# Reordering column turns, SyncE's requests and row loads in one layer of an attention and MLP kernel

## Chip, cores and metric

The kernel runs on one core of one Trainium2 chip. The metric is the device time of one launch in microseconds, the median of several runs; lower is better.

## What is computed

A routed attention block is followed by a small MLP with a layer norm and a residual sum. Only the second half matters here:

```python
B, H, S, D = 4, 8, 768, 64                  # x: (4, 768, 512)
x  = attention(q, k, v, centroids)          # softmax within clusters, per head
mu  = mean(x, -1); var = mean((x - mu)**2, -1)
xn  = (x - mu) / sqrt(var + 1e-6) * g_ln
out = x + maximum(xn @ w_ch1, 0) @ w_ch2    # w_ch1: 512 x 2048, w_ch2: 2048 x 512
```

Everything is in float32.

## The kernel before

The attention of all four sequences comes first and takes the span up to about 318 us. Then the MLP runs sequence by sequence, numbered b = 0 to 3. Matrix products are split with Strassen's method (seven products of half blocks instead of eight), the later ones twice over, so that between the products there are many sums and differences on VectorE.

The MLP's first layer of one sequence goes in eight **units**, j = 0 to 7, written by `first_units(b, j)` followed by `unit_end(b, j)`. A unit is a list of seven **parts** in the order 1, 2, 4, 6, 3, 5, 7, each one product of four matmuls with 128x384 results; parts 4 and 3 belong to the unit before. Parts 1, 6, 7 and 4 collect in one PSUM bank, `x_ps`: ScalarE copies its state out (`p1` after part 1, `u2` after part 6, `u3` after part 7, by `kept`, line 881) before the next part adds to it. Part 6 can therefore not start before the copy p1 is done, nor part 7 before u2. VectorE adds these copies to other banks (line 886), and ScalarE then applies the relu (line 894). In part 4 ScalarE applies the relu straight from the bank (line 923).

All five engines here take their instructions in the order in which the code issues them (a schedule written out by hand; SyncE, which issues most DMAs, included). So an instruction that waits holds up everything behind it on its engine.

Much else is tucked into the units of b = 1 and the stretch after it:

- **Rows of x for sequence 2.** `rows_load(2, t)` (line 560) fetches 128 rows of x (256 KB) from DRAM into a tile `xr`, of which there are two. `norm_rows(2, t)` (lines 573 to 575) lets ScalarE find their mean and spread. This is done at the ends of units 0 to 5, and each call requests the row block two further on once its own tile is free. From these, `norm_stats` and `norm_stat_rows` (at the ends of units 5 and 6) make the layer norm's factors: a small store `stat_d` to DRAM, and after it two loads that spread it over all partitions, `stat_row`.
- **Columns of x for sequence 3.** x lies in DRAM by columns. `columns_load` fetches 384 KB of it into `col` (line 534). `columns_turn` lets VectorE transpose it (line 518) and puts four stores of 96 KB into a list, `leaving`; they go to DRAM row by row in pieces of 128 bytes. `leave(n)` issues the first n of that list (line 1224). Turns stand at the ends of units 0, 2 and 4, loads at the ends of 1 and 3. Loaded and transposed tile share one pair of buffers.
- **Splits of the second weight.** At the end of each unit but the last, `w2_split(m, ...)` makes four differences on VectorE (line 1068) and stores 1 MB to DRAM, `w_d` (line 1069). `w2_back(i)` fetches 1 MB of earlier sums, `w_t`, at the ends of units 1, 3 and 4 (line 1047).
- **The ring.** The second layer ("deep" products, line 1151) takes its 49 weights of 256 KB, from `w_d`, `w_t` and `w_all`, through a ring of ten buffers. `ring_load` issues a load (line 1093); at the ends of units 5, 6 and 7 up to four each. The first products are named (4,1), (4,2), (4,6), (4,5), (4,7), (7,1) and so on.

The order in `unit_end` before the change is: row work, four of the leaving stores, the split with its store, `w2_back`, pending jobs, `norm_stats` and `norm_stat_rows`, leaving stores, column turn or load, ring loads. The same functions serve b = 2, whose first layer uses smaller products and takes about 13 us per unit; its row work already stands behind part 1.

Of the kernel before, what the change touches and what calls it, by code (L numbers as in the profile page):

```python
# [23 lines left out]
def kernel(  # L24
# [11 lines left out]
    nc = tc.nc  # L36
    B, H, S, D = q.shape
# [3 lines left out]
    NT = S // P  # L41
# [501 lines left out]
    rows = {}  # L543
# [11 lines left out]
            nc.sync.dma_start(out=xn[:, c, :], in_=xT_d[b][c])  # L555

    def rows_load(b, t):
        if t < NT:
            x = (ffn if b else last).tile([P, DM], F32, tag="xr", name="xr", bufs=2 + (not b))
            nc.sync.dma_start(out=x, in_=x_d[b][t])  # L560
            rows[b, t] = x

    def norm_rows(b, t):
        if b < 2:
            rows_load(b, t + 2 - b)
        x = rows.pop((b, t))
        if t == 0:
            moments[b] = small.tile([P, NT, 3], F32, tag="mv", name="mv")
        mv = moments[b]
        if b != 1:  # L570

            total, mean = mv[:, t, 0:1], mv[:, t, 1:2]
            nc.scalar.activation(x, x, AF.Identity, accum_out=total)
            nc.scalar.mul(mean, total, -1.0 / DM)
            nc.scalar.activation(x, x, AF.Square, bias=mean, accum_out=mv[:, t, 2:3])
            if b:
                rows_load(b, t + 2)
            return
        bn = small.tile([P, 6], F32, tag="bn", name="bn")
        nc.vector.bn_stats(out=bn, in_=x)  # L580
        nc.vector.bn_aggr(out=mv[:, t, :2], in_=bn)
# [350 lines left out]
    def by_half(w):  # L932

        return w.rearrange("p c (h f) -> p h c f", h=2)
# [126 lines left out]
    def w2_split(m, src):  # L1061

        blocks = [[src[:, j, l * NQH : (l + 1) * NQH] for j in range(2)] for l in range(2)]
        (b11, b12), (b21, b22) = blocks
        t = splits.tile([P, 4, NQH, P], F32, tag="wt", name="wt", bufs=2)
        t1, t2, t3, t4 = [t[:, i] for i in range(4)]
        for o, x, y in ((t1, b12, b11), (t2, b22, t1), (t3, b22, b12), (t4, b21, t2)):
            nc.vector.tensor_tensor(o, x, y, ALU.subtract)  # L1068
        nc.sync.dma_start(
            out=w2_d[ORDER.index(m)].rearrange("w p f -> p w f"), in_=t.rearrange("p w c f -> p w (c f)")  # L1070
        )

# [149 lines left out]
    def leave(n, queues=(nc.sync,)):  # L1222
        for i, (to, y) in enumerate(leaving[:n]):
            queues[i % len(queues)].dma_start(out=to, in_=y)
        del leaving[:n]
# [378 lines left out]
    def first_units(b, j):  # L1604

        chunks = within.pop(j, []) if b == 0 else []
        parts = ((1, 0), (2, 0), (4, 1), (6, 0), (3, 1), (5, 0), (7, 0))
        sums_after, inner_at = 5, {}
        if b >= PAIRED:
            parts = ((1, 0), (5, 0), (4, 1), (6, 0), (3, 1), (7, 0))  # L1610
            sums_after, inner_at = 3, {5: (7,), 6: (4, 3)} if j % 2 else {6: (1, 2), 7: (6, 5)}
            if j == 1:
                inner_at = {1: (1, 2), 6: (6, 5), 3: (7,), 7: (4, 3)}
        for part, ahead in parts:
            if chunks and part in (1, 3):
                split_weight(chunks[0])
            if j >= ahead:
                first_layer(b, j - ahead, part)
            if part in (4, 6, 3):
                relu(1)  # L1620
            if part in inner_at:
                inner_products(pairs_of[b, j - j % 2], inner_at[part])
                if 3 in inner_at[part]:
                    summed.extend(hidden_tile(0, j - i) for i in (1, 0))
                relu(len(summed))
            if inner_at and part == 1 and j % 2 == 0:
                if j == 2:
                    outer_sums(0, True)
                pair_begin(b, j)
            if inner_at and part == 1 and b + 1 < B and j < NT:  # L1630
                norm_rows(b + 1, j)
            if chunks and part in (2, 3):
                m = chunks.pop(0)
                join_weight(m)
                load_weight(m + RAWS)

            if part == sums_after and j + 1 < NFH:
                w1_sums(b, j + 1)
                if inner_at:
                    outer_keep(b, j + 1)  # L1640
            if inner_at and j % 2 and part in (1, 5):
                inner_keep(b, j - 1, {1: 5, 5: 3}[part])
            if part == sums_after and b and j:
                if not inner_at or j % 2 and j > 1:
                    outer_sums(j - 1, b > 1 or j > 4)
                if j + 1 == NFH and not inner_at:
                    inner_sums(deep[b], ORDER[0], cs=slice(0, NQH - 1))
            if inner_at and part == 7 and j % 2 == 0:
                outer_sums(j - 1, True)
# [82 lines left out]
    with tc.manual_schedule(engines=order | {mybir.EngineType.SP}):  # L1732
        first.close()
        splits = first.enter_context(tc.tile_pool(name="splits", bufs=1))
        outer = {}

        def unit_end(b, j):

            if b + 1 < B:
                if j == 0 and b < PAIRED:  # L1740
                    rows_load(b + 1, 1)
                if j < NT and (b < PAIRED or j == 0):
                    norm_rows(b + 1, j)
            if b == 1:
                leave(4)
                if j == 0:
                    outer["ends"] = all_in_range()
                if j == 2:
                    outer["flag"] = flag_of(outer.pop("ends"))
                m = (1, 5, 3, 4, 2, 7, 6, None)[j]  # L1750
                if m in SUMS:
                    w2_split(m, outer.pop(("t", SUMS.index(m) + 1)))
                elif m:
                    w2_split(m, by_half(w2_block(*{1: (0, 0), 2: (1, 0), 3: (1, 1)}[m])))
                if j in (1, 3, 4):
                    w2_back({1: 4, 3: 3, 4: 2}[j])
                if j in (5, 6):
                    outer_late("s", "e", (0, 0), j - 5)
            while pending:
                job = pending.pop(0)  # L1760
                if job is None:
                    break
                job()
            if b + 1 < B and j + 3 == NFH:
                norm_stats(b + 1)
            if b + 1 < B and j + 2 == NFH:
                norm_stat_rows(b + 1)
            leave(8 if b >= PAIRED else 4)
            if b == 1:
                if turning and j % 2 == 0:  # L1770
                    columns_turn(row, lambda out, in_: leaving.append((out, in_)))
                elif asked and j % 2:
                    columns_load(row)
            if j > 4:
                for _ in range(4):
                    if ring["next"] < len(STEPS) * (b - 1) + RING:
                        ring_load(b)

        for b in range(1, B):
            deep[b] = {}  # L1780
            if b + 1 < B:
                rows_load(b + 1, 0)
                if b >= PAIRED:
                    rows_load(b + 1, 1)
            if b == 1:
                w2_back(1)
                first_units(b, 0)
            elif b == LAST:
                last_load(3, 0)
                last_layer(b)  # L1790
            else:
                first_layer(b, 0, 6)
                w1_sums(b, 0, (2, 3))
                x_sum(b, 3)
                first_layer(b, 0, 5)
                x_sum(b, 4)
                first_layer(b, 0, 7)
                w1_sums(b, 1)
                deep_room(b)
                outer_keep(b, 0)  # L1800
                outer_keep(b, 1)
                pair_begin(b, 0)
            if b < LAST:
                unit_end(b, 0)
                for j in range(1, NFH):
                    first_units(b, j)
                    unit_end(b, j)
                relu(len(summed))
            if b == LAST:
                pass  # L1810
            elif b >= PAIRED:
                inner_sums(deep[b], ORDER[0], cs=slice(0, NQH - 1))
            else:
                inner_sums(deep[b], ORDER[0], cs=slice(NQH - 1, NQH))
            if b == 1:
                first.close()
                units = pool("units", 1)
            deep_layer(b, b + 1 < B, deep[b])
        flag = outer["flag"]
# [231 lines left out]
```

## Time and profile before

| What | us |
|---|---|
| Median of 3 runs | 879.64 |
| Lowest and highest run | 879.08, 880.81 |
| The profiled execution's own time | 880.61 |
| Its span, first to last instruction | 878.8 |
| TensorE (PE) busy in the span | 866.9 |
| VectorE (DVE) busy | 730.0 |
| ScalarE (ACT) busy | 408.0 |

In lines of the profile, PE is TensorE's matmuls, PEld its weight loads, DVE VectorE, ACT ScalarE, SP SyncE; a q after the name means the engine's sequencer, as for all DMA requests. A line of the timeline gives start, duration, engine, source line, operation, the tiles written and read, the shapes, and in brackets how long the engine had been idle and what ended that. A line of the waits gives who waited for whom, the sum in us, how often, and the longest. The first layer of b = 1 lies between 464 and 536 us, the second layer after it up to about 602 us.

### The profile page before, as it was taken

What the parts mean: (1) busy time and instruction counts of PE and PEld (TensorE: products, weight loads), DVE (VectorE), ACT (ScalarE), POOL (GpSimd) and SP (SyncE); (2) the same over time, 40 slices, a digit from 0 to 9 for tenths busy, and PEclk for the clock granted to TensorE, in tenths of its full rate; (3) what the DMA queues carried; (4) which work ended last, traced back from release to release, by engine and by line L of the source; (5) the groups of instructions that cost most, each with busy time, mean ns of one, the idle gap of its engine ahead of it and who ended that gap; (6) DMA issues with size and microseconds to landing.
All of it is one profiled execution on the core that took longest, in us unless ns stands there. A gap on an engine that the chain in (4) does not pass through costs nothing.

```text
span 878.8 us, 13640 instructions
## 1 busy us (share of the span) xinstructions
PE 866.9 (99%) x4744; PEld 586.4 (67%) x4744; DVE 730.0 (83%) x1262; ACT 408.0 (46%) x758; POOL 77.6 (9%) x143
## 2 busy tenths in 40 slices
PE   8999999999999999999999999999999999999996
PEld 5444444444444445568886557997667998778996
DVE  6899999999999888959667778897877897867875
ACT  6777788888888833330004452102553111443110
POOL 1012121222222212110000000000000000000000
PEclk9999999999999999999999999999999999999999
DMA  7777789999987328876685787965557875464875
GB/s 153 147 130 128 146 174 193 196 210 198 187 176 193 104 83 222 238 187 230 182 195 158 223 276 271 324 193 143 141 173 251 291 203 153 126 179 136 274 200 110
DMA packets 258493, 164.68 MB, mean 187 GB/s; under 512 B 192992, under 2 KB 211440, under 8 KB 257392
## 3 DMA queue, kind: packets, MB, share of 16 engines
q1 hardware_dynamic: 227392, 144.43, 60.7%
q0 software_dynamic: 7776, 15.03, 8.7%
q10 hardware_dynamic: 23248, 4.25, 2.8%
q8 instruction: 40, 0.66, 0.3%
q14 instruction: 37, 0.30, 0.1%
HBM read 115.21 MB, written 40.07 MB: 177 GB/s over the span
## 4 chain that ended last, share of the span: by engine, by line
PE 91%; DVE 3%; DMA 3%; ACT 1%; issue 1%; ACTq 0%; SPq 0%; DVEq 0%
PE s_ps L401 18%; PE x_ps L855 17%; PE a_ps L413 14%; PE x_ps L1151 11%; PE z_ps L855 6%; PE z_ps L1151 5%; PE x_ps L964 5%; PE y_ps L1151 3%; PE x_ps L1274 2%; PE z_ps L964 2%; PE y_ps L855 2%; PE sim_ps L320 1%; PE den_ps L469 1%; PE z_ps L1274 1%; PE y_ps L964 1%; DVE wt L1068 1%
## 5 line engine op out<-in xcount | busy, mean ns | idle before, releaser
L401 PE MATMUL s_ps<-t,t 64*128 64x384 f32 x768 | 154.8, 483 | 0.0
L401 PEld LDWEIGHTS s_ps<-t,t 64*128 64x128 f32 x768 | 68.0, 187 | 39.0 <-issue 38.3
L1151 PE MATMUL x_ps<-lower,w 128*128 128x192 f32 x448 | 80.8, 326 | 0.9 <-DVE u L1166 0.5
L1151 PEld LDWEIGHTS x_ps<-lower,w 128*128 128x128 f32 x448 | 74.1, 190 | 2.2 <-DVE u L1166 0.7
L396 ACT ACTIVATE e<-s_ps 128x768 f32<-128x768 f32 x84 | 67.1, 812 | 7.0 <-PE s_ps L401 6.4
L396 ACT ACTIVATE w<-s_ps 128x768 f32<-128x768 f32 x80 | 64.4, 813 | 8.3 <-PE s_ps L401 7.7
L894 ACT ACTIVATE lower<-lower 128x384 f32<-128x384 f32 x88 | 43.7, 520 | 51.8 <-DVE lower L886 37.7
L401 PE MATMUL s_ps<-mask,mask 64*128 64x384 bf16 x384 | 62.8, 323 | 1.0 <-ACT e L396 0.6
L881 ACT COPY u<-x_ps 128x384 f32<-128x384 f32 x64 | 30.6, 478 | 61.1 <-PE x_ps L855 61.0
L413 PE MATMUL a_ps<-e,v_sb 128*64 128x384 f32 x336 | 57.6, 488 | 0.0
L881 ACT COPY p<-x_ps 128x384 f32<-128x384 f32 x32 | 15.1, 473 | 86.5 <-PE x_ps L855 81.4
L413 PE MATMUL a_ps<-w,v_sb 128*64 128x384 f32 x320 | 55.2, 488 | 0.0
L855 PE MATMUL x_ps<-xt,ws 128*128 128x384 f32 x128 | 46.8, 488 | 0.9 <-ACT p L881 0.9
L855 PE MATMUL x_ps<-xn,w 128*128 128x384 f32 x128 | 46.6, 487 | 0.0
L855 PE MATMUL x_ps<-xn,ws 128*128 128x384 f32 x128 | 46.6, 487 | 0.0
L855 PE MATMUL x_ps<-xt,w 128*128 128x384 f32 x128 | 46.5, 486 | 0.0
L413 PEld LDWEIGHTS a_ps<-e,v_sb 128*64 128x64 f32 x336 | 23.5, 137 | 31.8 <-issue 29.3
L1506 POOL DMA_DIRECT2D out_dram<-y_end x2 | 1.2, 596 | 483.8 <-DVE y_end L1502 483.8
L413 PEld LDWEIGHTS a_ps<-w,v_sb 128*64 128x64 f32 x320 | 22.4, 137 | 30.4 <-issue 27.5
L401 PEld LDWEIGHTS <-mask 64*128 64x128 bf16 x384 | 18.9, 94 | 35.0 <-issue 10.0
L1164 ACT COPY u<-x_ps 128x192 f32<-128x192 f32 x30 | 9.6, 319 | 64.6 <-PE x_ps L1151 60.1
L886 DVE TENSOR_TENSOR lower<-z_ps,u 128x384 f32<-128x384 f32 x40 | 22.2, 555 | 20.6 <-PE z_ps L855 12.5
(296 smaller groups left out, 1834.7 us busy)
## 6 DMA issues: line engine op xcount, KB each, us to landing
w<-w_d SPq DMA_DIRECT2D x84, 256.0 KB, 3.3
raw<-in_moe_w_ch_dram SPq DMA_DIRECT2D x32, 512.0 KB, 4.5
w<-w_t SPq DMA_DIRECT2D x36, 256.0 KB, 5.4
w<-tb POOLq DMA_DIRECT2D x32, 256.0 KB, 5.7
w_d<-wt SPq DMA_DIRECT2D x7, 1024.0 KB, 5.9
w<-w_all SPq DMA_DIRECT2D x27, 256.0 KB, 3.0
v_sb<-in_v_dram SPq DMA_DIRECT2D x32, 192.0 KB, 3.6
xr<-x_d SPq DMA_DIRECT2D x24, 256.0 KB, 3.2
```

Source lines behind the costliest of these rows:

```text
L320: nc.tensor.matmul(sim[r : r + Q, :HC], cT[:, pr, :, :].rearrange("p j c -> p (j c)"), prepared[n][side][:, g * HC : (g + 1) * HC], start= ...
L396: nc.scalar.activation(e, s[:, :, :HC], AF.Exp, scale=SCALE)
L401: nc.tensor.matmul(s[:, j, :HC], of_keys[:, keys], of_queries[:, o : o + HC], start=part == first, stop=part != first, skip_group_check=True,)
L413: nc.tensor.matmul(acc[j * D : (j + 1) * D, :HC], loaded[n]["v"][:, j, c, :], e[:, j, :], start=(c == 0), stop=(c == NT - 1),)
L855: nc.tensor.matmul(bank[:, :HC], lhs[:, c, :], rhs[:, c], start=first and c == 0, stop=c == NDH - 1, skip_group_check=True,)
L881: nc.scalar.copy(t, bank[:, :HC])
L886: nc.vector.tensor_tensor(h, bank[:, :HC], other, ALU.add)
L894: nc.scalar.activation(h, h, AF.Relu)
L964: nc.tensor.matmul(bank[:, :MH].rearrange("p (h f) -> p h f", h=2), hidden[lhs + (c,)][:, tt * P : (tt + 1) * P], rhs[:, :, c], start=firs ...
L1151: nc.tensor.matmul(bank, w[:, c, :], a[:, c], start=way in (1, 2, 5) and c == 0, stop=c == NQH - 1, skip_group_check=True,)
L1164: nc.scalar.copy(o, rows_of(of))
L1274: nc.tensor.matmul(bank, p["w"][way], p["x"][way], start=way in (1, 2, 5), stop=True, skip_group_check=True)
```

## The change

The row work of b = 1 moves from the ends of units 1 to 5 to just behind part 1 of the same units, and each call now requests the next row block instead of the one after it; the first two are requested at the start. The column turns move to part 6 of units 1, 3 and 5, and the column loads go to the front of `unit_end`. The split's store is issued at the end of `unit_end` with `w2_back` after it, and the ring loads go ahead of the statistics. No instruction of PE, VectorE or ScalarE is added or taken away, and no DMA.

```diff
     def rows_load(b, t):
-        if t < NT:
+        if t < NT and (b, t) not in rows:
...
     def norm_rows(b, t):
-        if b < 2:
-            rows_load(b, t + 2 - b)
+        rows_load(b, t + 1 + (not b))
         x = rows.pop((b, t))
...
-            if b:
-                rows_load(b, t + 2)
             return
...
     # w2_split
-        nc.sync.dma_start(
+        return lambda: nc.sync.dma_start(
             out=w2_d[...], in_=t...
         )
...
     # first_units, after a part
-            if inner_at and part == 1 and b + 1 < B and j < NT:
+            if b and part == 1 and b + 1 < B and 0 < j < NT:
                 norm_rows(b + 1, j)
+            if b == 1 and part == 6 and j % 2 and turning:
+                columns_turn(row, lambda out, in_: leaving.append((out, in_)))
...
     # unit_end
             if b + 1 < B:
-                if j == 0 and b < PAIRED:
-                    rows_load(b + 1, 1)
-                if j < NT and (b < PAIRED or j == 0):
+                if j == 0:
                     norm_rows(b + 1, j)
             if b == 1:
                 leave(4)
+                if asked and j % 2:
+                    columns_load(row)
...
-                    w2_split(m, ...)
-                if j in (1, 3, 4):
-                    w2_back({1: 4, 3: 3, 4: 2}[j])
+                    split = w2_split(m, ...)
...
+            if j > 4:
+                for _ in range(4):
+                    if ring["next"] < len(STEPS) * (b - 1) + RING:
+                        ring_load(b)
             if b + 1 < B and j + 3 == NFH:
                 norm_stats(b + 1)
             if b + 1 < B and j + 2 == NFH:
                 norm_stat_rows(b + 1)
             leave(8 if b >= PAIRED else 4)
-            if b == 1:
-                if turning and j % 2 == 0:
-                    columns_turn(row, lambda out, in_: leaving.append((out, in_)))
-                elif asked and j % 2:
-                    columns_load(row)
-            if j > 4:
-                for _ in range(4):
-                    if ring["next"] < len(STEPS) * (b - 1) + RING:
-                        ring_load(b)
+            if b == 1 and m:
+                split()
+                if j in (1, 3, 4):
+                    w2_back({1: 4, 3: 3, 4: 2}[j])
...
     # start of a sequence's first layer
                 rows_load(b + 1, 0)
-                if b >= PAIRED:
-                    rows_load(b + 1, 1)
+                rows_load(b + 1, 1)
```

More of the change, by code (lines that the diff above doesn't have):

```diff
@@ L1751, in unit_end @@
                 if m in SUMS:
-                    w2_split(m, outer.pop(("t", SUMS.index(m) + 1)))
+                    split = w2_split(m, outer.pop(("t", SUMS.index(m) + 1)))
                 elif m:
-                    w2_split(m, by_half(w2_block(*{1: (0, 0), 2: (1, 0), 3: (1, 1)}[m])))
-                if j in (1, 3, 4):
-                    w2_back({1: 4, 3: 3, 4: 2}[j])
+                    split = w2_split(m, by_half(w2_block(*{1: (0, 0), 2: (1, 0), 3: (1, 1)}[m])))
                 if j in (5, 6):
```

## Prediction

> **What bounds the kernel now.** I read the head of the page first, then the waits of 464 to 560 us, where the second sequence's first layer lies, then the timeline there, because it alone gives starts.
>
> ```profile
> span 878.8 us, 13640 instructions
> PE 866.9 (99%) x4744; PEld 586.4 (67%) x4744; DVE 730.0 (83%) x1262; ACT 408.0 (46%) x758; POOL 77.6 (9%) x143
> ...
> PE x_ps L855 <- ACT p L881: 0.9, 2, 0.5
> PE x_ps L1151 <- DMA w<-w_d: 0.4, 1, 0.4
> DVE col L518 <- DMA col<-xT_d: 4.5, 1, 4.5
> DVE col L518 <- DMA w_d<-wt: 4.5, 1, 4.5
> ```
>
> PE sets the time; nothing elsewhere counts unless PE waits for it. In this layer it waits three times, 1.3 us by the records. Matmul ends are modelled, so I take starts. Part 1 of units 1 to 7 starts at 470.81, 479.84, 488.98, 498.01, 507.72, 516.75 and 526.66. A unit of 28 matmuls is 9.03; a small transpose (flag, statistics) adds 0.11 to units 2 and 6. What is left over is 9.71 - 9.03 = 0.68 in unit 4 and 9.91 - 9.03 - 0.11 = 0.77 in unit 6. At the third wait, the product before starts at 542.17 and is worth 1.30, the next starts at 544.07 (0.60 lost), and the two products there end 0.07 late besides: 0.67. **Together 2.12 us, 0.24% of the time. That is the most that this layer can give back.**
>
> The chain behind the first stall, from the timeline:
>
> ```profile
> 486.38 1.36 SPq L534 DMA_DIRECT2D col<-xT_d  x1
> ...
> 497.53 0.98 DVE L518 STREAM_TRANSPOSE col<-col 128x768 f32<-128x768 f32 x1 [4.50 <-DMA w_d<-wt]
> ...
> 498.98 0.99 ACT L894 ACTIVATE lower<-lower 128x384 f32<-128x384 f32 x2 [4.16 <-DVE lower L886]
> ...
> 500.23 0.64 ACT L573 ACTIVATE xr<-xr 128x512 f32<-128x512 f32 x1
> ...
> 501.94 0.46 ACT L881 COPY p<-x_ps 128x384 f32<-128x384 f32 x1
> ...
> 502.45 1.56 PE L855 MATMUL x_ps<-xt,ws 128*128 128x384 f32 x4 [0.41 <-ACT p L881]
> ```
>
> The column load goes out last, behind two transfers of 1 MB, and lands 10.9 us later (the DMA view of that issue), at 497.3; so it is the load, not the w_d that the view names, that ends VectorE's 4.50 us. ScalarE's relus wait for VectorE; behind them stands the row work (500.23 to 501.94), and only then p1, which PE needs for part 6. Unit 6 repeats this (load 9.3 us, transpose at 516.02, p1 at 520.77, PE at 521.28).
>
> The third stall is SyncE's queue:
>
> ```profile
> 531.85 0.37 SPq L1069 DMA_DIRECT2D w_d<-wt  x1
> 532.32 2.01 SPq L608 DMA_DIRECT2D stat_d<-st  x1
> ...
> 537.22 0.80 SPq L611 DMA_DIRECT2D stat_row<-stat_d  x2
> ...
> 538.08 0.42 SPq L1093 DMA_DIRECT2D w<-w_d  x1
> ...
> 544.07 2.84 PE L1151 MATMUL x_ps<-lower,w 128*128 128x192 f32 x16 [0.43 <-DMA w<-w_d]
> ```
>
> The ring load of product (4,7) stands behind a store that waits for VectorE and a broadcast that waits for the statistics' landing (532.32 to 537.22). It lands 5.9 us after 538.08.
>
> [...] p1's matmuls had started at 498.01, its copy ran at 501.94, after the row work. [...]
>
> **The change, part by part.**
>
> *Column turns.* Nothing is added: three transposes (0.98 each) and twelve stores move from the ends of units 0, 2, 4 to part 6 of units 1, 3, 5; two column loads (384 KB) move ahead of the unit's w_d and w_t requests. The first turn ends at about 479.0, so its four stores are issued 479.0 to 481.5 (2.5 us, as at 482.61), the load at 481.5 instead of 486.38. Ahead of it lie w_d (landed 481.9), one row and the stores (about 2.5 us of data): landing near 486, an estimate from these. It is wanted in unit 3 after the splits, at about 493.6, with 7 us to spare. The 4.5 us wait goes; the second likewise. VectorE then does per unit, by row durations: adds 1.5, split 2.64, sums 1.5, outer sums 1.1 to 1.5, transpose 0.98 in odd units, 0.95 more in unit 6: 7.7 to 8.3 of 9.03. It keeps up, and the transposes are covered by PE's matmuls.
>
> *Row work.* Five times 1.71 us of ScalarE (471.39 to 473.10) move from before p1 to just behind it; p1 then runs when its matmuls end. This alone takes the row work out of the 501.94 and 520.77 chains. **Gain of both: 0.68 + 0.77 = 1.45.**
>
> *Rows fetched later.* Row 1 is asked for sooner, beside row 0; the others pay. Before, row 3 was requested at 482.25 and used at 500.23. Now row 2 goes out behind w_d at 478.0 and is wanted at 481.8; row 3 behind w_d and w_t at about 486.3, wanted at 491.0; rows 4 and 5 at about 493.5 and 502.8, wanted at 500.0 and 509.0. From 4 to 6.5 us, where a row took 5.8 here. What is queued behind a late row on ScalarE: the relu of part 4, one of VectorE's relus, and u2, which part 7 needs 7.74 into the unit. Row work 1.71, relus 0.39 and 0.52, u2 0.48, semaphores 0.1: a row may land 4.5 into the unit before PE stops. Row 2: lands 482.6 (w_d's 481.9 and 256 KB at 380 GB/s), limit 484.4. Row 3: the data ahead (stores till 485, column till 486, w_d and w_t of 2.75 each at that rate) end about 492.2, the row at 493.0; limit 493.5. Rows 4 and 5: 498.5 and 510, limits 502.5 and 511.5. Row 3 is the close one. The trace doesn't show it: lower bound nothing lost (nor can a row that comes sooner than wanted gain anything); upper bound the column load's own 10.9 us from the same place, 497.2, a loss of 3.7. I take 0.1.
>
> *SyncE's order.* Seven w_d stores (waiting for VectorE), three w_t loads and w_d's wait go last in a unit; eight ring loads pass ahead of these and of stat_d. Load (4,7) then goes out near 521, lands before 530 and is wanted at 542: **gain 0.67.** Late next: nothing near; w_d of product 6, now behind stat_row, lands some 27 us before its use. SyncE's reading of the flag (0.8 us from 493.48) moves between stat_d and stat_row, into the 4.9 us that stat_d flies. w_t has over a unit of slack. The third sequence's layer gets the same order; 602 to 738 us shows PE without a gap, so nothing there, if rows asked for a unit ahead of 13 us land.
>
> **Sum** against the profiled execution's own 880.61 (span 878.8 and 1.8 around it): 880.61 - 1.45 - 0.67 + 0.1 = 878.59. The runs' median is 879.64, 0.97 below that execution, so 877.6. A measurement can tell about 0.2%, 1.76 us, from no change: the line is at 877.88, and the whole gain passes it by little.
>
> **Rivals.**
> - *A, all three stalls go, row 3 costs under 0.5: 877.6*, own range 877.2 to 878.2. For it: each stall has one visible cause, and each cause is moved by microseconds. 62%, 54 of them below 877.88.
> - *B, row 3 late by 0.5 to 3: 879.0* (877.5 + 1.5). For it: half a microsecond of slack on an estimate of 7. Against: stores and column leave the queue 3 us sooner. 14%.
> - *C, slower: 881.8.* Row 3's request, in the place where the column load took 10.9 us, takes as long: ScalarE stands until 497.2, PE loses 3.7 in unit 3, and row 5 with 9.3 us (512.1 against 511.5) 0.6: 877.5 + 4.3. It decides from a landing at 495.6, where the gain is eaten; past 497.4 it shows. Against it: part of those 10.9 us was the stores' data, now gone first. 16%.
> - *D, it doesn't do what it says: 879.6.* VectorE, 8.85 of 9 us busy at 500 to 509, stays behind without its idle stretches, and relus and p1 come as late as before. Against it: that busy stretch is the catching up after the 4.5 us. 8%.
>
> **How the numbers follow.** Likeliest 877.6. Faster by over 0.2%: 0.54 (of A). Within: 0.08 of A, B and D: 0.30. Slower: C, 0.16. Range 877.0 to 881.0: leaves out some 5% of A below and most of C above.
>
> **What would show it.** Right: part 1 starts 9.03 apart (9.14 twice) from unit 1 to 7; transposes with no wait for a DMA; ScalarE's p1 straight after its matmuls; ring loads before stat_d; no wait of PE for w_d. Wrong: a wait of ScalarE's L573-line work for xr in units 2 to 5 with PE's part 7 waiting for u2 (B, C), VectorE late without a DMA wait (D), or a new PE wait past 545 us.

## The result and the profile after

The changed kernel takes **881.02 us** (median of 22 runs, 879.65 to 885.38) beside 879.14 (22 runs, 878.13 to 880.81) of the kernel before: ratio 1.0025, 95% interval 1.0016 to 1.0034. It is slower by 1.9 us where a gain of 2.0 was forecast (877.6 beside the 879.64 of that time). The spread has grown as well: 16 of the 22 runs lie between 879.65 and 881.44, six between 882.2 and 885.4. The profiled execution of after is one of the six (884.5 us), so it shows the trouble larger than the median has it. Line numbers of after are three lower than those of before (L855 is L852, L881 is L878, L573 is L572).

The head of the page after:

```profile
span 882.7 us, 13640 instructions
PE 869.2 (98%) x4744; PEld 587.3 (67%) x4744; DVE 730.3 (83%) x1262; ACT 407.4 (46%) x758; POOL 77.6 (9%) x143
```

The work is the same, PE has the same 4744 matmuls, and yet it is busy 2.3 us longer than before (866.9). Waits alone would not do that, since a waiting engine does not count as busy (PE has 0.00 in the stretch of its wait, 497.10 to 499.50, in the view by stretches below). Now the waits of 464 to 570 us (sum, times, longest):

```profile
ACT xr L572 <- DMA xr<-x_d: 8.0, 3, 5.3
...
PE x_ps L852 <- ACT u L878: 2.4, 1, 2.4
...
DVE m L1163 <- DMA w_d<-wt: 1.3, 1, 1.3
```

All three waits of the prediction are gone: no PE behind p, no PE behind a ring load, no VectorE behind `col`. In their place stands one longer wait, and it is the one that the prediction named as the sign of failure: ScalarE for a row, PE's part 7 for u2. SyncE's timeline shows the request of row 3, the last line, and what goes out ahead of it:

```profile
479.20 4.29 SPq L1221 DMA_DIRECT2D x_d<-col  x4
483.53 0.55 SPq L534 DMA_DIRECT2D col<-xT_d  x1
485.15 0.38 SPq L1066 DMA_DIRECT2D w_d<-wt  x1
485.58 0.51 SPq L1044 DMA_DIRECT2D w_t<-w_t  x1
486.18 0.38 SPq L560 DMA_DIRECT2D xr<-x_d  x1
```

The timeline behind it, in unit 3:

```profile
490.69 0.48 ACT L878 COPY p<-x_ps 128x384 f32<-128x384 f32 x1 [0.92 <-PE x_ps L852]
...
496.49 0.63 ACT L572 ACTIVATE xr<-xr 128x512 f32<-128x512 f32 x1 [5.32 <-DMA xr<-x_d]
...
498.20 0.47 ACT L920 ACTIVATE lower<-x_ps 128x384 f32<-128x384 f32 x1
...
498.98 0.47 ACT L878 COPY u<-x_ps 128x384 f32<-128x384 f32 x1
...
499.50 2.80 PE L852 MATMUL x_ps<-xn,ws 128*128 128x384 f32 x4 [2.40 <-ACT u L878]
...
502.10 1.95 PE L852 MATMUL x_ps<-xn,w 128*128 128x384 f32 x4
```

ScalarE finished p1 at 491.17, took the row work next, and stood 5.32 us until the row landed. Behind that in its queue stood part 4's relu, whose matmuls had started at 493.07 and which ran at 498.20, and u2, for which PE waited 2.40 us by the records, 2.56 counted from start to start. Then something follows that no wait explains: four matmuls take 2.80 instead of 1.45. The view by stretches gives the length of each, the busy time and count of PE, weight loads, DVE, ACT and POOL, then PEclk (the clock that TensorE was granted, 1.00 for full speed), the busy share of the DMA engines, and GB/s:

```profile
495.00:497.10 2.10, 2.10 (x7) 0.95 (x5) 1.22 (x3) 0.61 (x2) 0.00 (x0) 1.00 1.00 285
497.10:499.50 2.40, 0.00 (x1) 0.00 (x1) 0.77 (x3) 2.33 (x9) 0.00 (x0) 1.00 1.17 284
499.50:503.30 3.80, 3.80 (x7) 2.11 (x8) 1.56 (x3) 1.26 (x3) 0.00 (x0) 0.55 0.66 140
503.30:506.00 2.70, 2.70 (x10) 1.64 (x9) 2.67 (x6) 1.86 (x5) 0.00 (x0) 1.00 0.00 0
```

After the pause PE's granted clock falls to a half: 0.55 is the mean over these 3.8 us, within which it is 0.50 from 499.67 to 503.08 and 1.00 on either side. Matmuls then start 640 ns apart, not 323, which costs another 1.80. In this execution the late row costs 2.56 + 1.80 = 4.36 us.

### The profile page after: what moved, and what is told of

It is laid out like the page before. It is cut to its first block, busy times and chain, and to the rows that moved or that the text cites. A ratio compares the mean times of both kernels' runs of the same rounds, so it can differ in the third digit from the quotient of the medians.

```text
span 882.7 us, 13640 instructions
## 1 busy us (share of the span) xinstructions
PE 869.2 (98%) x4744; PEld 587.3 (67%) x4744; DVE 730.3 (83%) x1262; ACT 407.4 (46%) x758; POOL 77.6 (9%) x143
## 4 chain that ended last, share of the span: by engine, by line
PE 93%; DMA 3%; DVE 1%; ACT 1%; SPq 1%; issue 0%; ACTq 0%; DVEq 0%
PE s_ps L401 17%; PE x_ps L852 17%; PE a_ps L413 14%; PE x_ps L1148 12%; PE z_ps L1148 6%; PE z_ps L852 6%; PE x_ps L961 5%; PE y_ps L1148 3%; PE z_ps L961 2%; PE x_ps L1271 2%; PE y_ps L852 2%; DMA xr<-x_d 2%; PE den_ps L469 1%; PE sim_ps L320 1%; PE y_ps L961 1%; PE z_ps L1271 1%
## 5 line engine op out<-in xcount | busy, mean ns | idle before, releaser
L878 ACT COPY u<-x_ps 128x384 f32<-128x384 f32 x64 | 30.6, 478 | 62.1 <-PE x_ps L852 61.8
L878 ACT COPY p<-x_ps 128x384 f32<-128x384 f32 x32 | 15.3, 477 | 91.1 <-PE x_ps L852 85.9
L852 PE MATMUL x_ps<-xn,ws 128*128 128x384 f32 x128 | 48.1, 499 | 2.4 <-ACT u L878 2.4
L852 PE MATMUL x_ps<-xn,w 128*128 128x384 f32 x128 | 47.1, 491 | 0.0
L852 PE MATMUL x_ps<-xt,ws 128*128 128x384 f32 x128 | 46.6, 487 | 0.0
L852 PE MATMUL x_ps<-xt,w 128*128 128x384 f32 x128 | 46.5, 486 | 0.0
L366 ACT ACTIVATE mask<-oh,far 32x384 bf16<-32x384 bf16 x61 | 37.3, 612 | 3.3 <-DVE oh L349 1.9
```

The lines of the kernel that those rows point to most:

```text
L366: nc.scalar.activation(out, oh[src, :], AF.Identity, bias=add, scale=factor)
L852: nc.tensor.matmul(bank[:, :HC], lhs[:, c, :], rhs[:, c], start=first and c == 0, stop=c == NDH - 1, skip_group_check=True,)
L878: nc.scalar.copy(t, bank[:, :HC])
```

## Experiments

Every kernel below was timed beside the kernel before. That kernel's median was 879.11 to 879.19 throughout, so that medians can be set against each other.

### The three parts, each alone

`turns_alone`: before, with the column part only.

```diff
     # first_units                              # unit_end, after leave(4)
+    if b == 1 and part == 6 and j % 2 and turning:
+        columns_turn(row, ...)
+                if asked and j % 2:
+                    columns_load(row)
```

> The kernel before with the column edit alone: turns in part 6 of units 1, 3, 5, column loads at the front of the unit's end. Theory: VectorE's two waits of 4.5 us go, with them the stalls of units 4 and 6 (0.68 and 0.77); the ring's wait (0.67) stays: 877.7 (877.4 to 878.2). Rival (the row work ahead of p1 is the cause, not the column): 878.7 to 879.2, stalls still there.

Measured: 878.81 (13 runs), ratio 0.9995, 0.9987 to 1.0003. Its trace shows no PE stall anywhere in the layer, and none for the ring load either. The time is the rival's, but without the rival's stalls: the edit does all that was asked of it, and the median is only 0.3 us below before. A second profile of the kernel before (`before_look`, below) tells why.

`rows_alone`: before, with row work behind part 1 and each row requested a unit later.

```diff
     def norm_rows(b, t):
-        if b < 2:
-            rows_load(b, t + 2 - b)
+        rows_load(b, t + 1 + (not b))
...
-            if b:
-                rows_load(b, t + 2)
```

> The kernel before with the row edit alone: row work behind part 1, each row asked for a unit ahead. Theory: rows now stand behind w_d, w_t and the column load too, row 3 lands 10 to 12 us after its request, ScalarE waits, PE stops some 2.5 to 4 us and runs at half clock behind it: 882 to 885, slower than the changed kernel. Rival (rows are harmless, the order costs): 878.5 to 879.5.

Measured: 881.52 (9 runs), ratio 1.0027, 1.0017 to 1.0037: less than the theory's 882 at least, far more than the rival's. The timeline of `rows_alone`:

```profile
496.10 0.63 ACT L572 ACTIVATE xr<-xr 128x512 f32<-128x512 f32 x1 [4.84 <-DMA xr<-x_d]
...
499.11 1.56 PE L852 MATMUL x_ps<-xn,ws 128*128 128x384 f32 x4 [1.92 <-ACT u L878]
```

The same wait in the same place, 2.08 from start to start, but the matmuls behind it take 1.56 for four: full clock (1.00 from 498 to 503 us), where the theory had the half.

`order_alone`: before, with SyncE's new order only (the edits of `w2_split`, `w2_back` and the ring loads).

> The kernel before with SyncE's order alone: w_d and w_t last in a unit, ring loads ahead of the statistics; turns and rows as before. Theory: the ring's wait goes (0.67), and since the column loads now go out ahead of w_d and w_t, the two waits for columns shrink too: 877.0 to 878.5, at least 0.6 below before. Rival (stores held back cost later, when the ring reads them): 879 or more, PE waiting for ring loads after 545 us.

Measured: 880.34 (13 runs), ratio 1.0013, 1.0005 to 1.0022. The part that was to save 0.67 costs 1.2. The rival has the time right but not the way: the trace has no wait of PE for a ring load. What costs is looked for in `order_look`, below.

`rows_early`: after, with sequence 2's rows requested two ahead again, behind ScalarE's work on the tile that comes free; the row work stays behind part 1.

```diff
-        rows_load(b, t + 1 + (not b))
+        if b != 2:
+            rows_load(b, t + 1 + (not b))
...
+            if b == 2:
+                rows_load(b, t + 2)
             return
```

> The changed kernel, but row j+2 of sequence 2 is asked for behind row j's statistics in unit j (as far ahead as before the change), not row j+1. Theory (the late row 3 stops ScalarE, then PE, and PE's clock halves for 3.4 us behind that pause): no wait of ScalarE for xr, no PE stall in unit 3, all three old stalls gone, about 2.1 us below before: 877.0 (876.6 to 877.6). Rival (the new order itself costs, by crowding transfers later, at 654 and at 786 to 806 us): 879 or more, with the losses there still in the trace.

Measured: 879.72 (13 runs), ratio 1.0006, 0.9997 to 1.0014. No wait for a row is left, PE has no stall in the layer, and 1.3 of the 1.9 us are back. The time at which the row is asked for is thus the main cost of the change. By the span (median over the runs) it is 879.15 - 877.6 = 1.55; the time outside of the span is 0.3 longer in this build and hides a part of it. The 877.0 of the theory is missed by 2.7 all the same. That is the rival's time; of the losses that the rival named, the trace shows one of 0.34 at 801 us, which comes again below.

### Were the three stalls the rule?

`before_look`: the kernel before once more.

> The kernel before once more, for a second profiled execution. If the first one (880.61, at the top of its runs) had its three stalls by chance, this one has fewer: a span near the usual 877.3, and stalls of 0.3 to 1.0 us in units 1 to 7 and at the ring instead of 2.12. If the stalls are the rule, they are here again, 2.1 us with a span of 878.8.

Measured: 878.87, span 877.1, and no stall at all in this layer, fewer than even the theory had. Its timeline in the place of the first stall:

```profile
496.31 0.98 DVE L518 STREAM_TRANSPOSE col<-col 128x768 f32<-128x768 f32 x1 [3.43 <-DMA col<-xT_d]
...
500.73 0.46 ACT L881 COPY p<-x_ps 128x384 f32<-128x384 f32 x1
...
501.74 1.45 PE L855 MATMUL x_ps<-xt,ws 128*128 128x384 f32 x4
```

VectorE still waits 3.43 us for the column, but it starts 1.22 earlier than in the first profile (497.53), p1 is 1.21 earlier, and PE's line has no bracket: it waited for nothing. One microsecond of landing decides between a stall of 0.68 and none. Set start against start, PE of the first profile runs 0.15 us behind this one up to 500 us, 2.27 at 546 us and 2.14 at 870: between 464 and 546 us the three stalls are the whole difference, and nothing makes up for them later. `ring_first` (below), whose turns, rows and splits stand as before, gives a third trace of the first two places: VectorE waits 3.5 and 3.8 us for columns there, and PE does not stall.

### A pause and the clock

`pause7` and `pause9`: `rows_early` with 7 or 9 more passes of ScalarE over row 3's tile in unit 3, in place and without effect on the values. They hold u2 back for a chosen time, with no DMA in it.

```diff
+            if (b, t) == (2, 3):
+                for _ in range(7):          # or 9
+                    nc.scalar.activation(x, x, AF.Identity)
```

> rows_early with seven more passes of ScalarE over row 3's tile in unit 3 (Identity in place, 0.65 us each, on a tile no longer read): 4.6 us more on ScalarE against about 2.7 us of slack, so PE stops about 1.9 us for u2. Theory [...]: full clock afterwards, time above rows_early by the pause alone, 881.5. Rival (any pause of PE brings the half clock, or it came by chance): the half clock here too, 1.8 us more.

> The same with nine passes: 5.9 us more, PE stops about 3.2 us. Theory: the granted clock falls to a half for some 3.4 us behind the pause, and the matmuls there lose 1.8 us beyond it: 879.7 + 3.2 + 1.8 = 884.7. Rival (the half clock in the changed kernel's profile was chance, or came from the transfers): the pause alone, 882.9.

Measured: 882.09 (6 runs) and 885.02 (3 runs). The timelines, first of `pause7`, then of `pause9`:

```profile
492.60 4.60 ACT L578 ACTIVATE xr<-xr 128x512 f32<-128x512 f32 x7
...
498.41 1.56 PE L858 MATMUL x_ps<-xn,ws 128*128 128x384 f32 x4 [1.61 <-ACT u L884]
```

```profile
492.43 5.92 ACT L578 ACTIVATE xr<-xr 128x512 f32<-128x512 f32 x9
...
499.57 2.93 PE L858 MATMUL x_ps<-xn,ws 128*128 128x384 f32 x4 [2.93 <-ACT u L884]
```

Two passes more, 1.32 us of ScalarE, cost 1.33 more of pause (3.10 instead of 1.77 from start to start) and another 1.74 in slow matmuls. From 499.5 to 503.3 us the granted clock is 1.00 in `pause7` and 0.55 in `pause9`, as in after. No row is late here, and the half clock came all the same behind the longer pause. By the idle records pauses of 1.61 and 1.92 (`rows_alone`) kept the full clock, 2.40 (after) and 2.93 lost it; no run has one between 1.92 and 2.40.

`after_look`: the changed kernel once more.

> The changed kernel once more, one look. Theory: its profiled execution of 884.5 was one of its slow ones. In a usual one (881.0) row 3 lands 9 to 10 us after its request, PE stops 1.0 to 2.1 in unit 3 for u2 and its clock stays full, so that the 1.8 us at half clock are missing: span 879 to 879.5. Rival: the half clock belongs to every execution: span 881 or more, with matmuls 640 ns apart behind the stop.

Measured: 879.3, span 877.5. Row 3 landed 8.4 us after its request:

```profile
494.40 0.63 ACT L572 ACTIVATE xr<-xr 128x512 f32<-128x512 f32 x1 [3.38 <-DMA xr<-x_d]
...
497.42 1.56 PE L852 MATMUL x_ps<-xn,ws 128*128 128x384 f32 x4 [0.46 <-ACT u L878]
```

PE lost 0.6 there, at full clock (1.00 from 497 to 504 us). The row landed sooner than the theory had it, and the rival falls: the half clock is no part of every execution. Over four traces row 3's flight, from request to landing, was 8.4, 8.7 (`rows_alone`), 9.5 (`after_store6`, below) and 10.3 us. This execution is faster than all 22 runs above, so no trace shows one near the median.

### Why SyncE's order costs, and where

`order_look`: `order_alone` once more, to find its loss.

> SyncE's order alone once more, for a second profiled execution; its first was one of its fastest. If holding back w_d and w_t costs in this layer, a usual run (span 878.5) shows PE stalls of about 1 us between 464 and 604 us, for columns or for ring loads. If it is the ring's place in the later sequences, they lie after 604 us.

Measured: 880.15, span 878.4. Both theories are half right: stalls of 0.35 + 0.10 at 542, and of 0.34 + 0.10 at 801, in the last layer. The timeline around the first:

```profile
526.32 0.38 SPq L608 DMA_DIRECT2D stat_d<-st  x1
...
532.67 0.81 SPq L611 DMA_DIRECT2D stat_row<-stat_d  x2
533.58 0.38 SPq L1069 DMA_DIRECT2D w_d<-wt  x1
...
540.95 0.36 DVE L1166 TENSOR_TENSOR m<-y_ps,p 128x192 f32<-128x192 f32 x1 [1.77 <-DMA w_d<-wt]
542.23 0.30 ACT L1164 COPY u<-x_ps 128x192 f32<-128x192 f32 x1
542.59 0.59 PE L1151 MATMUL x_ps<-lower,w 128*128 128x192 f32 x2 [0.19 <-ACT u L1164]
```

`m` neither reads nor writes `w_d`. It lies in memory that the tile `wt` has just given up, out of which the store still reads: VectorE waits for a buffer. In the new order unit 6's store stands behind stat_row, and stat_row waits for the landing of stat_d, which now has 1 MB of ring loads ahead of it: requested at 526.32, it let stat_row go at 532.67 only. So the store goes out at 533.58 instead of 529.94 (`before_look`).

`order_store6`: `order_alone` with this one store ahead of stat_d again.

```diff
+            if b == 1 and j == 6:
+                split()
             if b + 1 < B and j + 2 == NFH:
                 norm_stat_rows(b + 1)
...
             if b == 1 and m:
-                split()
+                if j != 6:
+                    split()
```

> The new order of SyncE's queue alone, but the last of the seven w_d stores (product 6's, unit 6) goes ahead of stat_d and stat_row again, with the ring loads still ahead of it. Theory: order_alone's PE stall of 0.35 + 0.10 at 542 comes from that store's buffer, which VectorE's first m of the next layer needs: behind stat_row the store went out at 533.2 to 533.6 instead of 529.9 and landed about 540.7, so m waited 1.5 to 1.8 us. Ahead of stat_d it goes out near 530, behind ring loads that landed by 532.6, and lands near 535: no wait of m for w_d<-wt, no PE stall at 542, about 0.4 less than order_alone: 879.9 where the kernel before gives 879.1. What is left over before is then the 0.45 at 801. Rival: the store is not what m waits for (rest_x or the ring loads end that wait): m still starts near 540.9, PE still stops 0.35 there and the time stays at 880.3.

Measured: 878.66 (21 runs), ratio 0.9992, 0.9986 to 0.9999. It is 1.7 below `order_alone`, more than the 0.4 expected, and the lowest median of all. Its timeline:

```profile
529.19 0.37 SPq L1069 DMA_DIRECT2D w_d<-wt  x1
...
538.77 0.35 DVE L1166 TENSOR_TENSOR m<-y_ps,p 128x192 f32<-128x192 f32 x1
...
541.92 1.30 PE L1151 MATMUL x_ps<-lower,w 128*128 128x192 f32 x7
```

The store lands at 535.56, `m` starts 2.2 us sooner and without a wait. The stall at 801 is gone too. It had its own sign, in the waits of `order_look` from 780 to 808:

```profile
DVE pi L1283 <- ACT u L881: 0.5, 1, 0.5
```

This line was in all seven traces of kernels that have the late store behind both stat_row and the ring loads, and in no other. VectorE's and ScalarE's lists of instructions at this place are the same with it and without it; why the wait comes is open. The two stalls make 0.9 of the 1.7; between these two traces the rest is in steps of 0.3 and less, some of them near the span's start.

`stores_last` is before with the stores and `w2_back` deferred alone, `ring_first` before with the ring loads moved alone.

> The kernel before with only the stores of w_d and the loads of w_t at the end of each unit's requests; the ring loads stay behind the statistics. Theory: the late store alone makes the stall at 542 (0.2 to 0.45), because it is still behind stat_row: 879.4 to 879.9 where the kernel before gives 879.1, with VectorE's m waiting for w_d<-wt. Rival: ring loads ahead of the store are what delays its landing (it flies 7 us behind 1 MB of them); without them it lands in 4.3 us as before, near 538, m does not wait, PE does not stop, and the time is that of before, 879.1.

> The kernel before with only the eight ring loads ahead of the statistics. Theory: the store keeps its early place, lands in time, and there is no stall at 542; nothing else is gained either since the ring wait of 0.67 was seen in one execution in two: 878.8 to 879.2 where the kernel before gives 879.1; whether VectorE's pi waits for ScalarE's u at 797 (0.45 of PE at 801) is open here: if it does, 879.5. Rival: ring loads ahead of the statistics themselves cost what order_alone costs (they delay stat_row or the next layer's xn loads): 880.0 to 880.3.

Measured: 879.25 (13 runs; 0.9989 to 1.0006) and 878.97 (13 runs; 0.9988 to 1.0005). The first is the time of the kernel before (879.19 beside it), as the rival had it, the second what the theory had. In `stores_last` stat_d, without the ring loads ahead, needs 3.4 us (526.26 to 529.70) instead of 6.4 until stat_row can go, so the store goes out at 530.61 and `m` doesn't wait. Neither half costs anything that can be measured; it takes the store behind stat_row and the ring loads ahead of both.

### Do the two causes add up?

`after_store6` and `early_store6`: the edit of `order_store6` made in after and in `rows_early`.

> The changed kernel with product 6's store ahead of stat_d again. Theory: the two causes stand side by side. order_alone lost 1.7 against order_store6, of which its trace shows 0.9 as stops of PE (0.45 at 542 and 0.45 at 801); in the changed kernel the store goes as well: 881.0 - 0.9 to 1.7 = 879.3 to 880.1 beside a kernel before of 879.1, with row 3's stop in unit 3 still there (0.6 to 2.6). Rival: the stop in unit 3 gives the store's load queue time to drain, so that the store costs nothing here: 881.0 stays.

> The changed kernel with the rows of the second sequence asked for two ahead and product 6's store ahead of stat_d again. Theory: both causes gone, nothing third: rows_early's 879.7 less 0.9 to 1.7 = 878.0 to 878.8, below the kernel before (879.1) and no PE stall between 464 and 604 nor at 801. Rival: a third cost remains in the combination, and it stays at rows_early's 879.7.

Measured: 881.19 (22 runs, 1.0013 to 1.0028) and 879.67 (13 runs, 0.9997 to 1.0013). Both rivals have the time right: in the changed kernel the early store gains nothing. The traces say how for the stall at 542: in the changed kernel `m` waited 0.6 and 1.3 us (`after_look`, after) and PE did not wait for it; at 1.8 (`order_look`) it did. Why the median shows nothing of the wait of `pi`, which is gone in `after_store6`, is open. Row 3's stop stays (in `after_store6` 1.79 from start to start).

`turns_store6`: `order_store6` with the edits of `turns_alone`, rows as before.

> The kernel before with the columns turned in part 6 and loaded first, and the new queue with product 6's store ahead of stat_d; rows as before. Theory: the 0.7 to 1.0 that early_store6 has over order_store6 belongs to the moved row work (its other places and its build), so that turns and queue together stay at the better of the two: 878.4 to 878.8 beside 879.2 of the kernel before, no PE stall in the layer. Rival: turns and queue hinder each other (two column stores and loads ahead of the store): 879.5 to 879.8.

Measured: 878.89 (13 runs), ratio 0.9999, 0.9991 to 1.0007, no stall in the layer. So turns and queue get on with each other. `early_store6`, which has the moved row work besides, lies 0.8 above it: 0.34 is the difference in time outside of the span (2.14 beside 1.80), 0.6 that in the span (877.6 beside 877.0); being medians, the two do not add up exactly. Neither was traced to a cause. The first cannot be put down to the row work: `rows_early` and `after_store6` have it too (2.15 and 2.11), after and `rows_alone` do not (1.86 both).

## Why the prediction was wrong

**The table of the difference**, by medians of the span (the kernel before: 877.3 to 877.4; the differences are from 877.4):

| Kernel | Span | Against before |
|---|---|---|
| turns_alone, turns_store6 | 877.0 | -0.4 |
| order_alone | 878.5 | +1.1 |
| order_store6 | 876.9 | -0.5 |
| rows_alone | 879.7 | +2.3 |
| rows_early, early_store6 | 877.6 | +0.2 |
| after, after_store6 | 879.1 | +1.7 |

The parts do not add up: alone they make -0.4 + 2.3 + 1.1 = 3.0, together 1.7. The missing 1.3 is about as much as the order costs alone; in the changed kernel that cost does not show.

**The sum, the first step that failed: the gain was not there to have.** The working took 2.12 us of stalls from the one execution that it had, 880.61, and then also the 0.97 by which that execution lay above the median. But those stalls are what put it there: a second profile, at 878.87, has none, and PE is 2.1 us ahead there for that reason alone. Each of the 2.12 was read rightly and belonged to that execution. What a kernel without them gains on the median is what `turns_alone` measured, 0.3 in time, 0.4 in span, less than can be told from nothing. The ring load's wait, too, is gone there without any change to SyncE's end of the queue. The lowest median of all variants is 878.66; 877.6 was reached by none. So of the 3.4 us between 877.6 and the measured 881.0, 1.5 were never there to gain (877.6 to 879.1); the other 1.9 are loss, most of it row 3's (below).

**The turns: right.** The column load left at 483.53, not at 481.5, since the four stores ahead of it held SyncE for 4.29 us and not 2.5; still no wait for the column is left, and VectorE keeps up. Rival D falls. The 2.5 was read at 482.61, when little else moved (158 GB/s from there to 485.1). Four such stores beside other transfers stood in the same trace, 517.02 to 521.06 at 274 GB/s, and took 4.04; the working itself had w_d in flight until 481.9.

**Row 3's landing, the second step that failed: it made the kernel slower.** The limit was good. PE stops, it said, if the row lands after 493.5; the landings at 494.4 and 496.5 cost 0.6 and 2.56, which puts the limit at 493.8 to 493.9. The request was right too, 486.18 for 486.3. The flight was taken as 6.7 us and was 8.4 to 10.3, and the cost as 0.1 where the spans' medians have 1.55. The estimate had w_d and w_t move at 380 GB/s (the first profile of before has 371 from 509 to 518 us and 404 from 493 to 495) and end at 492.2; the view by stretches shows 325 and 324 GB/s from 486 to 492 and 289 after, and w_t landed at 494.26, 8.7 us after its request. The row landed 2.2 us behind w_t in this trace and 0.6 in `after_look`, where 0.8 was planned; why it took so long here is open. The quickest of the 24 rows of this trace took 2.6 us from request to landing; what row 3 took beyond that, 5.8 to 7.7 us over the four traces, is put down to the transfers before and beside it, as an estimate. The prediction had this bound in hand: the column load's 10.9 us from the same place. It took 0.1 as the cost, because it held the stores and the column to be out of the way by then; they left SyncE 2 us later than it had them.

**Rivals B and C: the mechanism, in two sizes.** The wait, the engine and the part of PE are those named. The runs' median has B's size, 1.55 of span from after to `rows_early` in B's 0.5 to 3; the profiled execution has nearly C's flight, 10.3 of 10.9. That C's time, 881.8, lies near the measured 881.0 is luck: it starts from 877.5, 1.2 below the lowest median of any variant, and adds 4.3.

**What was not priced: the clock.** Loss was counted as pause for pause. Behind a pause of 2.40 us PE also restarted slowly, +1.80 here. The median does not hold this. The mean granted clock that each run lists is 0.996 in the three slowest of the 22 (884.5, 884.5 and 885.4) and 0.997 to 0.999 in all others, as in every run of the kernel before; the runs of `pause9`, whose trace has the half clock, list 0.995 and 0.996. 3.41 us at a half, 1.7 of a span of 882.7, take 0.002 off the mean by estimate, so the half clock is likely in three runs, of which one has a trace. The other three above 882 do not need it: the traced execution of `after_store6` took 882.44 at a mean clock of 0.998, with 1.56 us for the four matmuls behind its stop.

**SyncE's order: "late next: nothing near" was wrong.** It looked at who reads what the late store writes (w_d, 27 us later) and not at who needs the tile that the store reads. Alone the order cost 1.1 of span where 0.67 was forecast as gain, and `order_store6` shows that this one store is what costs. Of that cost the traces show 0.45 as the wait for the tile and 0.44 as the stall at 801, whose cause is open. In the changed kernel the cost does not show in the median.

## What to carry to other kernels

A stall seen in one execution is a sample: set that execution against the median first, and never take off both the stalls and the distance, for they may be one and the same. A transfer that is asked for later in a full queue is to be priced by the bytes ahead of it at the rate that the trace shows there (325 GB/s here, not 380), and the engine that waits for it by all that stands behind in its queue (part 4's relu and u2 behind 5.32 us here). A store that is put off holds its tile (`m` waited 1.77 us for one in `order_look`): look for the next owner of that memory, not only for the reader of the data. A pause of PE can cost more than its length: in after 2.56 us of it cost 4.36. The version to keep here is `order_store6`, by 0.5 us, which is less than a tenth of a per cent.

## What the hardware showed unexpectedly

Behind a pause of PE of 2.40 us in after the granted clock fell to 0.50. The trace's record of the clock has it so from 499.67 to 503.08, 3.41 us, beginning 0.17 after PE had resumed (499.50); from 4.73 to 499.67 and again from 503.08 to 878.55 it was full, the pause itself included. `pause9`, with a pause of 2.93, has the same mean of 0.55 over 499.5 to 503.3, and its four matmuls took 2.93.

The shorter pauses behind u2 kept the full clock: 0.46 us (`after_look`), 1.61 (`pause7`), 1.63 (`after_store6`) and 1.92 (`rows_alone`), with 1.56 us for the four matmuls behind each of them. Each of these lengths stands in one execution. Where between 1.92 and 2.40 the change lies, and whether the length of the pause alone decides it, no run shows.

SyncE's issue of four stores in pieces of 128 bytes took 2.53 and 2.49 us in the first profile of before while little else moved (158 and 160 GB/s), and 4.04 there and 4.29 in after beside other transfers (274 and 297 GB/s). Whether the other transfers decide it was not tried.
